# Exponentials of one PSUM bank in two halves, and of two banks in one operation, in a multi-query attention kernel

## The chip, the cores and the metric

The kernel runs on one core of a Trainium2 chip. The core has five engines with a queue of instructions each: TensorE (PE in the profile, with weight loads listed apart as PEld), VectorE (DVE), ScalarE (ACT), GpSimd (POOL) and SyncE (SP, which issues most of the transfers here). TensorE writes its products to PSUM, a memory of 128 partitions and eight banks of 512 float32 each; VectorE and ScalarE read them there and write to SBUF, the large on-chip memory. The metric is the device time of one execution in microseconds (us), lower being better.

## The reference, cut to what matters

A gated sum of two branches over one sequence of S = 2048 tokens of width D = 448:

```python
g = sigmoid((x * gate_w).sum(-1, keepdims=True))
a = A(x); b = B(x_b)
return g * a + (1 - g) * b

# A: multi-query attention, H = 16 heads of Dh = 28, one set of keys and values for all heads
q = (x @ wq).reshape(S, H, Dh)
k, v = x @ wk, x @ wv
p = softmax(einsum("qhd,kd->hqk", q, k) * Dh ** -0.5)
a = einsum("hqk,kd->qhd", p, v).reshape(S, H * Dh) @ wo

# B: spatial shift mixing and a feed-forward block
hs = shift4(gelu(layernorm(x) @ w1)) @ w2
x1 = x + hs
b = x1 + gelu(layernorm(x1) @ w3) @ w4      # 448 -> 1792 -> 448
```

All is float32. The change lies in the attention: the scores, the exponentials and the products with the values. 16 heads times 2048 queries times 2048 keys are 67 million exponentials.

## The kernel before, in words

Three stages follow each other. Stage 1 projects queries, keys and values (the queries wait in DRAM) and does the shift mixing. Stage 2 is the feed-forward block. Stage 3, from about 403 us to the end, is the attention and the output projection. The order of the instructions on every engine is the order in which the program writes them (a manual schedule); the semaphores between engines are set by the framework from what each instruction reads and writes.

**Attention.** The queries are in 16 units `u`: a block of 512 queries times a group of four heads. For one unit the 2048 keys come in 16 key tiles of 128. For one key tile, `scores` (L204) makes four products, one per head, in three rounds (high times high, low times high, high times low parts, to keep float32 precision). Each lands in a PSUM bank of its own: 128 keys by 512 queries. The four heads of a round run side by side on TensorE, each on 32 rows. The exponentials (`exps`, L257) read the banks and write the tile `p` in SBUF. `values` (L893) multiplies `p` with the values; it takes p as the moving operand, 256 queries at a time, and leaves the four heads' results in the four quarters of the partitions.

**The eight banks.** Four are single tiles, named `s0`, `s1`, `s2`, `s3_`; four form two pairs of banks, `pairs[0]` and `pairs[1]`. A pair is a tile of 128 x 2 x 512 read by one operation. From cycle to cycle `s0, s1` and `s2, s3_` change places.

**A cycle.** One pass through the main loop (index `c`, 128 of them) takes two key tiles. For TensorE it is written in this order:

1. scores of the first key tile into `s0`, `s1` and the two banks of `pairs[0]`;
2. scores of the second key tile into `s2`, `s3_` and the two banks of `pairs[1]`;
3. value products of the *previous* cycle's two tiles for queries 0 to 255, into the left half of `s0` (32 matmuls in all with step 4);
4. the same for queries 256 to 511, into the left half of `s1`;
5. usually one job (L844): half of an output projection of an earlier unit, into the right half of `s0`. In one cycle of each unit, row maxima of the next unit come between 3 and 4, into `pairs[0]` (L211).

For ScalarE the cycle before the change is: exponential of `s0` (`left`), of `s1` (`right`), of `s2`, of `s3_`, of `pairs[1]` (1024 columns, `both`), and then of the half of the first tile's `p` that VectorE has copied from `pairs[0]` to SBUF (L954), in place. That is six operations: four of 128x512 and two of 128x1024.

VectorE copies `pairs[0]` to SBUF, adds the value products to the running sums of the unit (`values_end`, L818; L814 the first time), once for step 3 and once for step 4, and adds the job's product (L860).

Step 3 writes to the bank `s0` that this cycle's first exponential reads, and step 5 writes to the bank that VectorE's first addition reads.

**Where the single banks come from.** Stages 1 and 2 use them too, through `mm_tile` (two buffers in turn, for the gate products of the feed-forward block among others) and `misc_tile` (one). `max_tile` gives the fourth. At the end of stage 2 they are made the four `singles`.

**Marked blocks.** In two cycles (`HINTS`, c = 68 and c = 110) the first exponential stands in a block of its own, which serves a hint for the later branch to the fallback path (that path recomputes everything with exact maxima, and isn't taken here).

Of the kernel before, what the change touches and what calls it, by code (L numbers as in the profile page):

```python
# [9 lines left out]
F32 = mybir.dt.float32  # L10
F32R = mybir.dt.float32r
BF16 = mybir.dt.bfloat16
AF = mybir.ActivationFunctionType
# [4 lines left out]
P = 128  # L18
# [11 lines left out]
SCALE = DH ** -0.5  # L30
# [12 lines left out]
def gated_mix_kernel(  # L43
# [12 lines left out]
    nc = tc.nc  # L56
# [3 lines left out]
    psA = ctx.enter_context(tc.tile_pool(name="psA", bufs=1, space=PSUM))  # L60
# [22 lines left out]
    nc.gpsimd.memset(vext[:, :, 0:1], 1.0)  # L83
    nc.gpsimd.memset(f32(kl), 1.0)

    def mm_tile(name):
        return psA.tile([P, 512], F32, tag="mm", bufs=2, name=name)

    def misc_tile(name):
        return psA.tile([P, 512], F32, tag="misc", bufs=1, name=name)  # L90

    def max_tile(name):
        return psA.tile([P, 512], F32, tag="mx", bufs=1, name=name)

    wps = misc_tile("warm_ps")
    for _ in range(20):
# [156 lines left out]
            for p in range(4):  # L253
                nc.sync.dma_start(rows[p], mrow[32 * p + 16 * k:32 * p + 16 * k + 16, :])

    def exps(p, heads, source=None):
        nc.scalar.activation(p[:, heads], p[:, heads] if source is None else source, AF.Exp, scale=SCALE)  # L257

    ctx2 = ExitStack()

# [1 line left out]
    with tc.tile_pool(name="s1b", bufs=1) as s1b, \  # L262
# [231 lines left out]
        q0 = first_queries()  # L494
# [172 lines left out]
    with tc.tile_pool(name="s2", bufs=1, reuse_waits="tile") as s2, \  # L667
# [35 lines left out]
        for b in range(NB):  # L703
            acc = [ps2.tile([P, 512], F32, tag="acc", bufs=4, name=f"acc_{b}_{t}") for t in range(4)]
            gs = {}
            for f in range(NF):
                if f == 9 and b + 1 < NB:
                    mv, rs = layernorm_stats(s2a, b + 1)
                if f == 10 and b + 1 < NB:
                    xt4 = big(f"xt4_{b + 1}")[:, 0:4 * D].rearrange("p (f t j) -> p f t j", f=NE, t=4)  # L710
                if f in (10, 11) and b + 1 < NB:
                    for t in (2 * f - 20, 2 * f - 19):
                        xn = s2a.tile([P, 512], F32, tag="xn", bufs=1, name=f"xn_{b + 1}_{t}")[:, 0:D]
                        layernorm_norm(b + 1, t, mv, rs, xn, xt4)
                if f == 11 and b + 1 < NB:
                    xt_write(b + 1, xt4)
                    ln_read(b + 1)
                gs[f] = w3_part(b, f)
                if b == 0 and f % 2 and f < 11:
                    split_w3((f + 3) // 2)  # L720
                    split_w4((f + 3) // 2)
                    if f == 1:
                        s2.tile([P, 48], F32, name="gap2")
                    if f < 9:
                        load_w34((f + 5) // 2, s2)
                if b == 1 and f == 0:
                    nc.gpsimd.tensor_tensor(gg, invE, gz, ALU.pow)
                    nc.vector.tensor_scalar(gg, gg, 1.0, None, op0=ALU.add)
                    nc.vector.reciprocal(gg, gg)
                    nc.vector.tensor_scalar(gi, gg, -1.0, 1.0, op0=ALU.mult, op1=ALU.add)  # L730
                if b == NB - 1 and f == 4:
                    weigh_x1(0, 4 * b)
                if b == 1 and f == 1:
                    nc.gpsimd.memset(khd, 0.0)
                    for j in range(4):
                        h = slice(32 * j, 32 * j + DH)
                        nc.gpsimd.tensor_copy(khd[h, j * MK:(j + 1) * MK], f32(kh_of[0])[h, 0:MK])
                    qr0 = s2a.tile([P, 512], F32, tag="xn", bufs=1, name="qr_0")
                    nc.gpsimd.memset(qr0, 0.0)
                    q_load(0, qr0)  # L740
                    nc.sync.dma_start(w4_late, w4[F - P:F, :])
                if b == 1 and f == 5:
                    q_high(0, qh0, ql0)
                    q_low(0)
                if f >= 2:
                    for t in range(4):
                        w4_part(f - 2, t, gs[f - 2], acc)
                        if b > 1 and t % 2 == 0 and f < NF - 1:
                            fill()
            if b == NB - 1:  # L750
                singles = [mm_tile("bank_0"), mm_tile("bank_1"), misc_tile("bank_2"), max_tile("bank_3")]
                scores(0, 0, singles)
                nc.scalar.activation(first, powt, AF.Exp)
                p_first = big("p_0_0").rearrange("p (j n) -> p j n", j=4)
                for j in range(4):
                    exps(p_first, slice(j, j + 1), singles[j].unsqueeze(1))
            for t in range(4):
                w4_part(NF - 2, t, gs[NF - 2], acc, NF - 2 if b == NB - 1 else NF - 1)
                if b + 1 < NB:
                    ln_split(b + 1, t, t + 1)  # L760
            for t in range(4):
                if b < NB - 1:
                    w4_part(NF - 1, t, gs[NF - 1], acc)
                xt = x1[:, 4 * b + t, :]
                nc.vector.tensor_add(xt, xt, acc[t][:, 0:D])
# [4 lines left out]
    with tc.tile_pool(name="s3", bufs=1, reuse_waits="tile") as s3, \  # L770
# [128 lines left out]
        left, right, both, front = slice(0, 1), slice(1, 2), slice(2, 4), slice(0, 2)  # L899
# [25 lines left out]
        for c in range(NC):  # L925
            u, i = divmod(c, NT // 2)
            k = 2 * c
            s0, s1, s2, s3_ = singles if c % 2 == 0 else singles[2:] + singles[:2]
            if c == 0:
                pb = score_tiles(u, 1, s2, s3_, s0, s1)  # L930
                for j, ps in enumerate((s2, s3_, s0, s1)):
                    exps(pb, slice(j, j + 1), ps.unsqueeze(1))
                pa = score_tiles(u, 2, *(q[:, h] for q in pairs for h in range(2)))
                nc.vector.tensor_copy(pa[:, front], pairs[0])
                for ps, n in zip((s2, s3_), JOBS_0):
                    run_jobs(ps, n)
                exps(pa, both, pairs[1])
                exps(pa, front)
                pairs.reverse()
                continue  # L940
            if c > 1:
                pa = score_tiles(u, 2 * i, s0, s1, pairs[0][:, 0], pairs[0][:, 1])
                with tc.block() if c in HINTS else nullcontext():
                    if c in HINTS:
                        tc.mark_branch_hint_location("redo", "LikelyTaken", HINTS[c])
                    exps(pa, left, s0.unsqueeze(1))
                exps(pa, right, s1.unsqueeze(1))
            if i == 2 and u == 0:
                q_begin(1)
            if i == 3 and u == 0:  # L950
                q_low(1)
                q_fetch(2)
            if 1 < c < NC - 1:
                nc.vector.tensor_copy(pa[:, both], pairs[0])  # L954
            elif c > 1:
                exps(pa, both, pairs[0])
            if i == 3 and later:
                later.pop(0)()
            if i == 1 and sums:
                norms.append(recip(*sums.pop()))  # L960
            if i == (3 if u == NU - 1 else 4) and norms:
                w = norms[0][0]
                norm(*norms.pop())
            if i == 5 and u + 2 < NU:
                q_begin(u + 2)
            if i == 6 and u + 2 < NU:
                q_low(u + 2)
                q_fetch(u + 3)
            pb = score_tiles(u, 2 * i + 1, s2, s3_, pairs[1][:, 0], pairs[1][:, 1])
            exps(pb, left, s2.unsqueeze(1))  # L970
            exps(pb, right, s3_.unsqueeze(1))
            exps(pb, both, pairs[1])
            if 1 < c < NC - 1:
                exps(pa, both)
            if u and i == (3 if u == NU - 1 else 4):
                jobs += [(wo_products, wo_add, (u - 1, t), cols) for t in range(4) for cols in halves]
            v = (c - 1) // (NT // 2)
            at_max = i == MAX_AT and u + 1 < NU
            q0, q1 = slice(0, 256), slice(256, 512)
            values((k - 2, k - 1), s0[:, q0], q0)  # L980
            values_end(v, s0[:, q0], q0)
            if at_max:
                max_part(u + 1, range(4), pairs[0][:, 0])
                later.append(lambda u=u: max_end(u + 1))
            elif i == MAX_AT:
                run_jobs(pairs[0][:, 0], 1)
            values((k - 2, k - 1), s1[:, q0], q1)
            adds = job_products(s0[:, q1], 0 if c in IDLE or c == 1 else 1)
            values_end(v, s1[:, q0], q1)
            job_adds(adds)  # L990
            if i == 0 and v < NU - 1:
                sums.append(sums_begin(v))
# [152 lines left out]
```

## Time and profile before

| what | value |
|---|---|
| time, median of 3 runs | 911.5 us (911.43 to 911.81) |
| span of the profiled execution, first to last instruction | 909.7 us |
| instructions | 24149 |
| TensorE matmul rows busy | 903.1 us, 99% |
| ScalarE busy | 632.6 us, 70% |
| VectorE busy | 515.8 us, 57% |
| granted TensorE clock, mean | 0.999 |
| attention, 128 cycles | about 403 to 899 us |
| ScalarE busy between 500 and 800 us | 99.64 to 99.75 us in each 100 us |

The profiled execution's time is given by its span; the runs' times include what lies before the first and behind the last instruction, and their median is 1.8 us above the span. How to read the rows: an instruction row of a timeline gives start and length in us, engine, line, operation, the tiles written and read, the shapes, how many were merged into the row, and in brackets how long the engine was idle before it and which instruction ended the idle time. PE's rows show matmuls in the pipeline, where several stand at once; PEld's rows show the loads of their weights, which go ahead of the matmul. A row of waits gives who waited, for whom, the sum in us, how many times, and the longest. ScalarE's operations overlap too: the next one starts before the end of the last.

### The profile page before, as it was taken

The page shows a single profiled execution, that of the slowest core. Times are in us where ns is not written, and L with a number is a line of the kernel's source. Part 1 is how long each engine was busy: PE and PEld are TensorE (multiplying, and loading weights), DVE is VectorE, ACT ScalarE, POOL GpSimd, SP SyncE. Part 2 cuts the span into 40 slices and gives each one's busy share as a digit, 9 for nine tenths or more (in the row PEclk, how much of TensorE's full clock was granted, in tenths as well). Part 3 has the DMA queues.
Part 4 walks back from the last instruction along what each step waited for, and adds up shares of the span by engine and source line. Part 5 has one row for each costly group of instructions (what it writes and reads, how often), then busy time and mean ns, then how long its engine had stood idle before and what let it go on. Part 6 is the DMA issues. An engine that isn't in the chain of part 4 may idle for free.

```text
span 909.7 us, 24149 instructions
## 1 busy us (share of the span) xinstructions
PE 903.1 (99%) x10360; PEld 626.8 (69%) x10360; DVE 515.8 (57%) x960; ACT 632.6 (70%) x1003; POOL 79.1 (9%) x116
## 2 busy tenths in 40 slices
PE   9999999999999999999999999999999999999998
PEld 6788888888888888875555555555555555555554
DVE  3665273631441531136766777676767667767665
ACT  5542444332132231269999999999999999999995
POOL 3243320200000520020000000000000000000000
PEclk9999999999999999999999999999999999999999
DMA  8832653120110120010000001000011000010001
GB/s 294 289 103 61 147 167 129 37 70 1 39 49 2 22 65 1 1 52 24 14 25 14 24 15 56 23 25 17 25 33 36 24 14 25 15 55 14 15 14 44
DMA packets 40726, 47.31 MB, mean 52 GB/s; under 512 B 10152, under 2 KB 28904, under 8 KB 40616
## 3 DMA queue, kind: packets, MB, share of 16 engines
q1 hardware_dynamic: 37448, 40.43, 15.2%
q10 hardware_dynamic: 3168, 5.31, 1.6%
q8 instruction: 82, 1.34, 0.6%
q14 instruction: 28, 0.23, 0.1%
HBM read 32.56 MB, written 11.67 MB: 49 GB/s over the span
## 4 chain that ended last, share of the span: by engine, by line
PE 97%; ACT 2%; DMA 1%; DVE 0%; issue 0%; SPq 0%
PE bank L893 26%; PE bank L204 20%; PE bank L844 6%; PE acc L701 5%; PE acc L699 5%; PE acc L700 5%; PE g L135 4%; PE g L137 4%; PE g L136 4%; PE pair L204 2%; ACT p L257 2%; PE hs L475 1%; PE hs L476 1%; PE g L138 1%; PE g L139 1%; PE h L136 1%
## 5 line engine op out<-in xcount | busy, mean ns | idle before, releaser
L257 ACT ACTIVATE p<-bank 128x512 f32<-128x512 f32 x514 | 265.9, 605 | 4.4 <-POOL pick L866 1.5
L893 PE MATMUL bank<-p,vext 128*32 128x256 f32 x4064 | 247.7, 382 | 1.0 <-ACT p L257 1.0
L893 PEld LDWEIGHTS bank<-p,vext 128*32 128x32 f32 x4064 | 117.9, 110 | 115.9 <-ACT p L257 53.0
L954 DVE COPY p<-pair 128x1024 f32<-128x1024 f32 x125 | 153.0, 1224 | 57.9 <-PE pair L204 40.9
L689 ACT ACTIVATE gh<-g 128x512 fp32r<-128x512 f32 x55 | 32.9, 598 | 181.7 <-PE g L139 181.7
L818 DVE TENSOR_TENSOR o<-o,bank 128x256 f32<-128x256 f32 x222 | 93.5, 421 | 80.4 <-PE bank L893 72.3
L257 ACT ACTIVATE p<-p 128x1024 f32<-128x1024 f32 x126 | 138.0, 1096 | 0.0
L257 ACT ACTIVATE p<-pair 128x1024 f32<-128x1024 f32 x129 | 136.8, 1060 | 0.0
L691 DVE TENSOR_TENSOR gl<-gf,gh 128x512 fp32r<-128x512 f32 x55 | 38.6, 702 | 164.9 <-ACT gf L690 164.9
L204 PE MATMUL bank<-qh,kh 32*128 32x512 f32 x514 | 114.8, 443 | 0.0
L204 PE MATMUL pair<-qh,kh 32*128 32x512 f32 x510 | 114.0, 443 | 0.0
L204 PE MATMUL bank<-qh,kl 32*128 32x512 f32 x514 | 101.8, 389 | 0.0
L204 PE MATMUL bank<-ql,kh 32*128 32x512 f32 x514 | 101.6, 390 | 0.0
L204 PE MATMUL pair<-qh,kl 32*128 32x512 f32 x510 | 101.3, 389 | 0.0
L204 PE MATMUL pair<-ql,kh 32*128 32x512 f32 x510 | 100.9, 389 | 0.0
L204 PEld LDWEIGHTS bank<-qh,kh 32*128 32x128 f32 x514 | 48.0, 182 | 61.3 <-issue 38.7
L701 PE MATMUL acc<-w4h,gl 128*128 128x448 f32 x220 | 80.7, 367 | 0.0
L699 PE MATMUL acc<-w4h,gh 128*128 128x448 f32 x220 | 80.2, 364 | 0.0
L700 PE MATMUL acc<-w4l,gh 128*128 128x448 f32 x220 | 79.8, 363 | 0.0
L844 PE MATMUL bank<-wof,on 128*32 128x224 f32 (+1 forms) x984 | 69.6, 357 | 0.0
L135 PE MATMUL g<-ah,w3h 128*128 128x512 f32 x168 | 65.4, 389 | 0.0
L136 PE MATMUL g<-al,w3h 128*128 128x512 f32 x168 | 65.4, 389 | 0.0
(206 smaller groups left out, 1394.1 us busy)
## 6 DMA issues: line engine op xcount, KB each, us to landing
qd<-qf ACTq DMA_DIRECT2D x15, 256.0 KB
rb<-rd SPq DMA_DIRECT2D x15, 256.0 KB
x<-in_x_dram SPq DMA_DIRECT2D x4, 896.0 KB
xd<-xt SPq DMA_DIRECT2D x16, 224.0 KB
w34raw<-in_w_dram SPq DMA_DIRECT2D x7, 512.0 KB
qr<-qd SPq DMA_DIRECT2D x64, 56.0 KB
w34raw<-in_w_dram SPq DMA_DIRECT2D x7, 448.0 KB
out_dram<-ot SPq DMA_DIRECT2D x14, 224.0 KB
```

Source lines behind the costliest of these rows:

```text
L135: nc.tensor.matmul(ps, wh[:, c, :], ah[:, c, :], start=(c == 0), stop=False)
L136: nc.tensor.matmul(ps, wh[:, c, :], al[:, c, :], start=False, stop=False)
L204: nc.tensor.matmul(ps[j], k[h, keys], q[h, :], start=(r == 0), stop=(r == 2), tile_position=(32 * j, 0))
L257: nc.scalar.activation(p[:, heads], p[:, heads] if source is None else source, AF.Exp, scale=SCALE)
L691: nc.vector.tensor_sub(gl, gf, f32(gh))
L699: nc.tensor.matmul(ps, gh[:, tok], w4h[i][:, k, :], start=(f == 0), stop=False)
L700: nc.tensor.matmul(ps, gh[:, tok], w4l[i][:, k, :], start=False, stop=False)
L701: nc.tensor.matmul(ps, gl[:, tok], w4h[i][:, k, :], start=False, stop=(f == stop))
L818: nc.vector.tensor_add(o, o, pv)
L844: nc.tensor.matmul(ps[32 * i:32 * i + 32, :], a[:, c:c + 32], w, start=start, stop=stop, tile_position=(0, 32 * i))
L893: nc.tensor.matmul(pv[32 * j:32 * j + 32, :], vext[:, kt, :], p_of[k][:, j, qs], start=(k == ks[0]), stop=(k == ks[-1]), tile_position=(0, ...
L954: nc.vector.tensor_copy(pa[:, both], pairs[0])
```

## The change

The four single banks become two tiles of two banks (`duo_0`, `duo_1`), of which `mm_tile`, `misc_tile` and `singles` are halves. In a cycle's ScalarE order, the first operation (bank `s0`, 512 queries) becomes two operations of 256 queries each, `q0` and `q1`. The third and the fourth (banks `s2` and `s3_` of the second key tile) become one operation over the two-bank tile that they form. The number of operations per cycle stays six: two of 128x256, one of 128x512, three of 128x1024. In the marked blocks only the first half remains inside; the second half follows the block. The last cycle reads `pairs[0]` directly as before.

```diff
+    duos = [psA.tile([P, 2, 512], F32, name=f"duo_{i}") for i in range(2)]
+    mm_turn = [0]
+
     def mm_tile(name):
-        return psA.tile([P, 512], F32, tag="mm", bufs=2, name=name)
+        mm_turn[0] += 1
+        return duos[0][:, 1 - mm_turn[0] % 2]
 
     def misc_tile(name):
-        return psA.tile([P, 512], F32, tag="misc", bufs=1, name=name)
-
-    def max_tile(name):
-        return psA.tile([P, 512], F32, tag="mx", bufs=1, name=name)
+        return duos[1][:, 0]
...
-    def exps(p, heads, source=None):
-        nc.scalar.activation(p[:, heads], p[:, heads] if source is None else source, AF.Exp, scale=SCALE)
+    def exps(p, heads, source=None, qs=slice(0, 512)):
+        nc.scalar.activation(p[:, heads, qs], p[:, heads] if source is None else source, AF.Exp, scale=SCALE)
...
-                singles = [mm_tile("bank_0"), mm_tile("bank_1"), misc_tile("bank_2"), max_tile("bank_3")]
+                singles = [d[:, h] for d in duos for h in range(2)]
...
             s0, s1, s2, s3_ = singles if c % 2 == 0 else singles[2:] + singles[:2]
+            duo = duos[1 - c % 2]
+            q0, q1 = slice(0, 256), slice(256, 512)
...
                 with tc.block() if c in HINTS else nullcontext():
                     if c in HINTS:
                         tc.mark_branch_hint_location("redo", "LikelyTaken", HINTS[c])
-                    exps(pa, left, s0.unsqueeze(1))
+                    exps(pa, left, s0[:, q0].unsqueeze(1), q0)
+                exps(pa, left, s0[:, q1].unsqueeze(1), q1)
                 exps(pa, right, s1.unsqueeze(1))
...
             pb = score_tiles(u, 2 * i + 1, s2, s3_, pairs[1][:, 0], pairs[1][:, 1])
-            exps(pb, left, s2.unsqueeze(1))
-            exps(pb, right, s3_.unsqueeze(1))
+            exps(pb, front, duo)
             exps(pb, both, pairs[1])
...
-            q0, q1 = slice(0, 256), slice(256, 512)
             values((k - 2, k - 1), s0[:, q0], q0)
             values_end(v, s0[:, q0], q0)
```

## The prediction

> **What bounds the kernel now.** I read the page's share table first, then the groups of instructions for the stretch 445 to 875 us (attention in its steady state), then the waits of that stretch, and then the timeline of two cycles at 609 us. On the page TensorE's matmul row is busy almost throughout. That alone decides nothing, since a matmul that stands in the pipeline counts as busy.
>
> ```profile
> span 909.7 us, 24149 instructions
> PE 903.1 (99%) x10360; PEld 626.8 (69%) x10360; DVE 515.8 (57%) x960; ACT 632.6 (70%) x1003; POOL 79.1 (9%) x116
> ```
>
> The waits between 445 and 875 us (engine and tile that waited, whom it waited for, us in total, times, longest) show where TensorE stands still:
>
> ```profile
> PEld bank L893 <- ACT p L257: 45.4, 110, 0.4
> PEld bank L204 <- issue: 34.3, 96, 0.4
> PEld bank L844 <- DVE o L818: 18.4, 83, 0.3
> ```
>
> One cycle of the loop handles two key tiles. The second row names no other engine ("issue" is time without a wait that the profile shows); the third is taken up below. 430 us hold 110 waits of the value products (L893) for an exponential, so there is one in every cycle and a cycle takes 430/110 = 3.91 us. The timeline of one cycle tells which exponential it is. The first row is the last operation of the cycle before. The single operations come from narrow windows; the row with x4 is the same four together.
>
> ```profile
> 608.08 1.09 ACT L257 ACTIVATE p<-p 128x1024 f32<-128x1024 f32 x1
> 608.72 0.40 PE L204 MATMUL pair<-qh,kl 32*128 32x512 f32 x2
> 609.14 0.60 ACT L257 ACTIVATE p<-bank 128x512 f32<-128x512 f32 x1
> 609.14 2.07 ACT L257 ACTIVATE p<-bank 128x512 f32<-128x512 f32 x4
> 609.42 0.39 PE L204 MATMUL bank<-qh,kl 32*128 32x512 f32 x1
> 609.64 0.59 ACT L257 ACTIVATE p<-bank 128x512 f32<-128x512 f32 x1
> 609.79 1.45 PEld L893 LDWEIGHTS bank<-p,vext 128*32 128x32 f32 x32 [0.41 <-ACT p L257]
> 610.11 0.61 ACT L257 ACTIVATE p<-bank 128x512 f32<-128x512 f32 x1
> 610.59 0.62 ACT L257 ACTIVATE p<-bank 128x512 f32<-128x512 f32 x1
> 611.07 1.06 ACT L257 ACTIVATE p<-pair 128x1024 f32<-128x1024 f32 x1
> 611.97 1.09 ACT L257 ACTIVATE p<-p 128x1024 f32<-128x1024 f32 x1
> 613.03 0.60 ACT L257 ACTIVATE p<-bank 128x512 f32<-128x512 f32 x1
> 613.68 0.16 PEld L893 LDWEIGHTS bank<-p,vext 128*32 128x32 f32 x8 [0.40 <-ACT p L257]
> ```
>
> The first key tile's scores end at 608.72 + 0.40 = 609.12. ScalarE starts on bank s0 at 609.14 and ends at 609.74. The value products, whose result goes into the left half of that same bank, load their first weights at 609.79, 0.05 us later. In the next cycle it is again 613.03 + 0.60 = 613.63 and 613.68. So the cycle is a ring: scores into s0, exponential of s0, value products into s0, output products, next scores. Whatever the exponential of s0 lasts longer or shorter, each cycle does too, as far as the rest of TensorE's work allows it.
>
> How much of that wait is real is seen where nothing has to be waited for. In an early cycle ScalarE was done with s0 at 406.33 + 0.60 = 406.93, long before the products:
>
> ```profile
> 406.33 0.60 ACT L257 ACTIVATE p<-bank 128x512 f32<-128x512 f32 x1
> 406.88 0.39 PE L204 MATMUL pair<-qh,kl 32*128 32x512 f32 x2
> 407.20 0.42 PE L893 MATMUL bank<-p,vext 128*32 128x256 f32 x4
> ```
>
> There the products start 407.20 − 406.88 = 0.32 us after the last scores. In the steady cycle it is 609.79 − 609.42 = 0.37. Only 0.05 us per cycle is lost to the exponential, though the wait row says 0.41.
>
> ScalarE itself has some room. From the operation on the tile in SBUF to the next cycle's first exponential are 609.14 − 608.08 = 1.06 us; where ScalarE is the one that is late, 417.98 − 417.03 = 0.95 us do:
>
> ```profile
> 417.03 1.09 ACT L257 ACTIVATE p<-p 128x1024 f32<-128x1024 f32 x1
> 417.98 1.12 ACT L257 ACTIVATE p<-bank 128x512 f32<-128x512 f32 x2
> ```
>
> **The change, part by part.** *Two halves in place of the first exponential.* The question is which of the halves the value products wait for. They write columns 0 to 255 of s0, and the second half reads columns 256 to 511 of the same bank. The kernel already has such a pair: the output products (L844) write columns 256 and up of s0, while VectorE (L818) has columns 0 to 255 to read.
>
> ```profile
> 610.99 0.42 DVE L818 TENSOR_TENSOR o<-o,bank 128x256 f32<-128x256 f32 x1
> 611.46 0.22 PEld L844 LDWEIGHTS bank<-wof,on 128*32 128x32 f32 x8 [0.22 <-DVE o L818]
> ```
>
> 610.99 + 0.42 = 611.41, and 0.05 us later L844 begins. It shares no column with L818, takes nothing that L818 makes, and still waits for it; the wait row above has it 83 times. So in this program order is kept by bank, not by column, and the value products will wait for the second half as well. The split then lengthens the ring by the cost of one more operation.
>
> The Trainium skill, "PSUM — Partial Sum Buffer", section "PSUM bank collisions raise a hardware error", says the same from the chip's side: two engines on one bank and the same 32 partitions at once is an error even at different columns, so one has to guard by bank. It speaks against the change; the trace's wait of L844 agrees.
>
> How much is it? No 128x256 exponential stands in the trace, so I take it from the two sizes that do. Start to start, operations of 512 follow each other at 610.59 − 610.11 = 0.48 us and one of 1024 is followed after 611.97 − 611.07 = 0.90. The 512 further elements take 0.42, so 256 take 0.21, and an operation has 0.48 − 0.42 = 0.06 us of its own. The first after a pause is followed after 0.50, 0.02 more. The first half is thus followed after 0.27 to 0.29 us, the second half lasts 0.59 − 0.21 = 0.38, and both end 0.65 to 0.67 after the start, where the single operation ended after 0.60. I take 0.06 us per cycle, the whole of one operation's own share.
>
> Both bounds: the least is 0.05. The most is what it would be if the halves did not overlap at all, which other operations of this kernel show (64 partitions, out of SBUF):
>
> ```profile
> 116.32 0.40 ACT L112 CAST w3h<-w34raw 64x256 fp32r<-64x256 f32 x1
> 116.74 0.41 ACT L113 CAST w3l<-w34raw 64x256 fp32r<-64x256 f32 x1
> ```
>
> The second starts 0.42 after the first, whose length is 0.40. Then the halves end 0.38 + 0.02 + 0.38 = 0.78 after the start: 0.18 more. That these two read one bank is no reason to expect it, for the two activations after the gate product also read one bank and overlap:
>
> ```profile
> 354.19 0.60 ACT L689 ACTIVATE gh<-g 128x512 fp32r<-128x512 f32 x1 [3.83 <-PE g L139]
> 354.69 0.59 ACT L690 ACTIVATE gf<-g 128x512 f32<-128x512 f32 x1
> ```
>
> The Trainium skill, "ScalarE: Activation LUTs", section "What ACT_TABLE_LOAD costs", gives 186 ns and 0.833 ns per element, of which back-to-back operations overlap by about 93 ns. By it one more operation is an estimated 0.093 us, and the sum below would be 11 us instead of 7. The trace is nearer to 0.06 at both sizes.
>
> *One operation for the second tile's two banks.* It takes away one start: two of 0.48 become one of 0.90, 0.06 us less. ScalarE's work per cycle is therefore what it was. But these operations come behind the gating one, and their results are used in the next cycle. Nothing waits for them at the end of the ring, so the 0.06 won here only goes to ScalarE's room of 0.11. The joint operation must wait for the scores of both banks. Those are complete at 609.42 + 0.39 = 609.81, and ScalarE gets there at about 610.11 + 0.05. It frees the first bank later, at about 610.16 + 1.06 = 611.22; the next scores into that bank start at 612.04:
>
> ```profile
> 612.04 0.49 PE L204 MATMUL bank<-qh,kh 32*128 32x512 f32 x2
> ```
>
> 0.8 us of cover, so this costs nothing. Without that cover scores would start late, by what the joint operation ends behind them.
>
> *The banks as halves of two tiles.* The feed-forward part uses the same two banks in turn, the score stage the same four. No operation, transfer or queue entry is added. If order is kept by bank, this costs nothing; what it costs otherwise is a rival below. The two marked blocks now hold the first half alone. After the later one ScalarE's operations follow without a gap (the second and third end 1.58 us after the first's start, 0.48 + 0.48 + 0.62), so I add nothing.
>
> ```profile
> 878.94 1.58 ACT L257 ACTIVATE p<-bank 128x512 f32<-128x512 f32 x3 [0.35 <-PE pair L204]
> ```
>
> **What is late next.** Value products 0.06 later move VectorE's additions and L844 with them, and the output products end 0.06 later, and so do the next scores. VectorE's copies wait for scores, ScalarE's room only grows. Nothing I see gives the time back.
>
> **The sum.** The value products' wait has 126 cases over the attention:
>
> ```profile
> PEld bank L893 <- ACT p L257: 53.0, 126, 0.7
> ```
>
> In some five early cycles like that at 417.98 ScalarE is late and the next start does not depend on TensorE, so I count 120. 120 × 0.06 = 7.2 us on the profiled span of 909.7, that is 916.9. The runs' median of 911.5 lies 1.8 us above this span; I keep that difference, and get 918.7 us.
>
> **The rivals.**
> 1. *Order by column.* If the products wait for the first half alone, that ends about 0.38 after its start, before TensorE is ready, and the products start at their own limit: 0.05 less per cycle, 120 × 0.05 = 6 us, 905.5 us. ScalarE's room of 0.11 would suffice. Against it stands L844's wait in 83 cases; for it, nothing in this trace. This is the other side, and it decides from the point where the products start ahead of the second half's end.
> 2. *Halves without overlap*: 120 × 0.18 = 21.6, 933 us. For it the 64-partition pair, against it all exponentials and the pair at 354 us.
> 3. *Order by tile.* If both banks of a joint tile count as one, the value products wait for s1's exponential too, which now ends at about 0.27 + 0.27 + 0.61 = 1.15 after the start instead of 0.60: 0.55 × 120 = 66 us, 977 us or more, as the feed-forward banks would be coupled as well. No row of the trace shows one bank of a two-bank tile written while the other is being read, so nothing speaks for or against.
> 4. *Nothing moves*: a later start of the products is taken up somewhere, 911.5 us. Against it: in two successive cycles they follow the exponential by the same 0.05 us, and TensorE has no other wait that could shrink.
>
> **How the numbers follow.** My forecast has 0.82, order by column 0.06, no overlap 0.04, order by tile 0.03, nothing moves 0.05. The forecast's own range is 0.05 to 0.09 us per cycle and a count of 115 to 126, with a little for what I have not seen: 916 to 924. The unknown price reaches toward rival 2 above and something given back below, so I widen it to 914 to 926, where about eight in ten lie. No change means within 0.2%, 1.8 us, about what a measurement of this kernel can tell. Faster is rival 1, 0.06; same is rival 4 and a price under a quarter of mine, 0.06; slower is the rest, 0.88.
>
> **What would show it.** In the changed profile there should be some 126 exponentials of 128x256 for each half, the second starting 0.27 to 0.29 us after the first and the value products 0.05 us after the end of the *second*. Their distance from the last scores should be 0.43 instead of 0.37, the cycle 3.97 instead of 3.91. Some 127 exponentials of 128x1024 from the joint tile stand in place of two of 128x512. If the products start before the second half ends, order is by column and I am wrong in sign; if they wait for the third operation, it is by tile; if the second half starts 0.4 after the first, the price was wrong.

## The result and the profile after

The changed kernel takes 1109.3 us (median, 1109.2 to 1109.7) against 911.5 us for the kernel before on the same chip: a ratio of 1.217, 95% interval 1.215 to 1.218. It is 198 us slower; 7 us were forecast.

The share table of the changed kernel's page:

```profile
span 1107.3 us, 24103 instructions
PE 971.1 (88%) x10360; PEld 613.7 (55%) x10360; DVE 519.5 (47%) x960; ACT 636.6 (57%) x1002; POOL 80.0 (7%) x116
```

The work is the same: as many matmuls, as many VectorE operations, ScalarE 636.6 us busy instead of 632.6 with one operation less. What grew is waiting. Four of the waits between 500 and 1000 us (engine and tile that waited, whom for, us in total, times, longest); the lines are one further down than before, so L894 is the value products, L819 VectorE's addition of them, L845 the job, L861 the addition of the job, L205 the scores and L258 the exponentials:

```profile
DVE o L819 <- PE duo L845: 126.3, 83, 1.6
PEld duo L894 <- DVE o L819: 84.5, 83, 1.1
PEld duo L894 <- ACT p L258: 66.3, 95, 0.7
PEld duo L205 <- DVE ot L861: 41.7, 95, 0.4
```

Of these only the third was in the profile before, but for two waits of the last kind, 0.4 us together. The value products now wait for VectorE, VectorE's additions wait for the job, and scores wait for the addition of the job. One cycle's timeline shows each (start, length, engine, line, tiles, and in brackets the idle time and what ended it):

```profile
702.84 0.50 PE L205 MATMUL duo<-qh,kh 32*128 32x512 f32 x2
703.32 0.45 DVE L861 SCALAR_TENSOR_TENSOR ot<-duo,gg,ot 128x224 f32<-128x224 f32 x1
703.81 0.18 PEld L205 LDWEIGHTS duo<-qh,kh 32*128 32x128 f32 x2 [0.44 <-DVE ot L861]
703.84 0.66 ACT L258 ACTIVATE p<-duo 128x256 f32<-128x256 f32 x2 [1.34 <-PE pair L205]
704.39 1.52 ACT L258 ACTIVATE p<-duo 128x512 f32<-128x512 f32 x2
705.04 1.07 PE L894 MATMUL duo<-p,vext 128*32 128x256 f32 x16 [0.26 <-ACT p L258]
706.24 0.42 DVE L819 TENSOR_TENSOR o<-o,duo 128x256 f32<-128x256 f32 x1 [0.53 <-ACT p L258]
706.71 1.07 PE L894 MATMUL duo<-p,vext 128*32 128x256 f32 x16 [0.60 <-DVE o L819]
707.60 0.56 PE L845 MATMUL duo<-wof,on 128*32 128x224 f32 x8
708.09 0.51 PE L205 MATMUL duo<-qh,kh 32*128 32x512 f32 x2
708.23 0.42 DVE L819 TENSOR_TENSOR o<-o,duo 128x256 f32<-128x256 f32 x1 [1.57 <-PE duo L845]
```

Read with the order of the program: the two halves of the exponential of s0 end at 703.84 + 0.66 = 704.50. The value products into s0 do not start then. They start at 705.04, 0.05 us after the exponential of **s1**, which starts at 704.39 and lasts 0.60 (the second row of ScalarE holds it and the joint operation, which starts at 704.87). The second part of the products, which goes into s1, waits until VectorE has read s0: 706.24 + 0.42 = 706.66, start at 706.71. VectorE's addition from s1 waits until the job has been written beside it into s0: 707.60 + 0.56 = 708.16, start at 708.23. s0 and s1 are now two banks of one tile, and whoever writes one of them waits for whoever uses the other. That is rival 3 of the prediction, with its sign and the kind of its mechanism, at three times its price.

The cycle is 708.09 − 702.84 = 5.25 us, where 3.91 were read before. The value products of the first cycles start at these times, before and changed:

```profile
403.47 0.42 PE L893 MATMUL bank<-p,vext 128*32 128x256 f32 x4
```

```profile
428.13 1.07 PE L894 MATMUL duo<-p,vext 128*32 128x256 f32 x16
```

So 24.7 us of the 197.6 us of span are lost ahead of the attention, where the projections of the first stage and the gate products of the feed-forward part share the same tiles, 169 us in the attention cycles (5.25 − 3.91 = 1.34, times 126), and the remaining 4 us behind the start of the last cycle's value products (18.4 us to the end of the span instead of 14.5). In the experiments below, one of the four runs of the last kernel had a granted clock of 0.75 and took 1195.5 us; it is left out of that kernel's time.

### The profile page after: what moved, and what is told of

It reads as the page before. It is cut to its first block, busy times and chain, and to the rows that moved or that the text cites. A ratio compares the mean times of both kernels' runs of the same rounds, so it can differ in the third digit from the quotient of the medians.

```text
span 1107.3 us, 24103 instructions
## 1 busy us (share of the span) xinstructions
PE 971.1 (88%) x10360; PEld 613.7 (55%) x10360; DVE 519.5 (47%) x960; ACT 636.6 (57%) x1002; POOL 80.0 (7%) x116
## 3 DMA queue, kind: packets, MB, share of 16 engines
q8 instruction: 82, 1.34, 0.5%
## 4 chain that ended last, share of the span: by engine, by line
PE 79%; ACT 11%; DVE 6%; issue 3%; DMA 1%; DVEq 0%; SPq 0%; ACTq 0%; POOL 0%
PE duo L894 21%; PE duo L205 18%; ACT p L258 9%; PE duo L136 5%; PE duo L845 5%; DVE o L819 4%; PE duo L137 4%; PE duo L138 4%; PE acc L702 4%; PE acc L700 4%; PE acc L701 4%; PE duo L140 1%; PE duo L139 1%; PE hs L476 1%; PE hs L477 1%
## 5 line engine op out<-in xcount | busy, mean ns | idle before, releaser
L894 PE MATMUL duo<-p,vext 128*32 128x256 f32 x4064 | 271.9, 385 | 109.4 <-DVE o L819 64.9
L258 ACT ACTIVATE p<-duo 128x256 f32<-128x256 f32 (+2 forms) x513 | 265.6, 603 | 171.2 <-PE pair L205 155.0
L894 PEld LDWEIGHTS duo<-p,vext 128*32 128x32 f32 x4064 | 106.0, 109 | 264.2 <-DVE o L819 112.9
L819 DVE TENSOR_TENSOR o<-o,duo 128x256 f32<-128x256 f32 x222 | 93.5, 421 | 264.1 <-PE duo L845 161.8
L258 ACT ACTIVATE p<-p 128x1024 f32<-128x1024 f32 x126 | 135.1, 1072 | 0.0
L258 ACT ACTIVATE p<-pair 128x1024 f32<-128x1024 f32 x129 | 134.0, 1039 | 0.0
L205 PE MATMUL duo<-qh,kh 32*128 32x512 f32 x514 | 126.3, 492 | 0.3
L205 PE MATMUL pair<-qh,kh 32*128 32x512 f32 x510 | 125.7, 491 | 0.0
L205 PEld LDWEIGHTS duo<-qh,kh 32*128 32x128 f32 x514 | 47.1, 181 | 99.7 <-DVE ot L861 50.5
L205 PE MATMUL pair<-qh,kl 32*128 32x512 f32 x510 | 100.8, 391 | 0.0
L205 PE MATMUL duo<-qh,kl 32*128 32x512 f32 x514 | 100.8, 390 | 0.0
L205 PE MATMUL duo<-ql,kh 32*128 32x512 f32 x514 | 100.7, 390 | 0.0
L205 PE MATMUL pair<-ql,kh 32*128 32x512 f32 x510 | 100.4, 390 | 0.0
L136 PE MATMUL duo<-ah,w3h 128*128 128x512 f32 x168 | 66.3, 395 | 9.4 <-ACT gf L691 9.4
L845 PE MATMUL duo<-wof,on 128*32 128x224 f32 (+1 forms) x984 | 70.1, 357 | 2.2 <-DVE ot L861 1.6
L137 PE MATMUL duo<-al,w3h 128*128 128x512 f32 x168 | 65.5, 390 | 0.0
```

The costliest lines, as they stand in the source:

```text
L136: nc.tensor.matmul(ps, wh[:, c, :], ah[:, c, :], start=(c == 0), stop=False)
L137: nc.tensor.matmul(ps, wh[:, c, :], al[:, c, :], start=False, stop=False)
L205: nc.tensor.matmul(ps[j], k[h, keys], q[h, :], start=(r == 0), stop=(r == 2), tile_position=(32 * j, 0))
L258: nc.scalar.activation(p[:, heads, qs], p[:, heads] if source is None else source, AF.Exp, scale=SCALE)
L819: nc.vector.tensor_add(o, o, pv)
L845: nc.tensor.matmul(ps[32 * i:32 * i + 32, :], a[:, c:c + 32], w, start=start, stop=stop, tile_position=(0, 32 * i))
```

## The experiments

Each kernel stands against the kernel before on the same chip (911.6 us). "Start to start" below is the distance between two starts in the same cycle, the median over 126 cycles, worked out from the start times in the trace.

| kernel | us | ratio to before, 95% interval |
|---|---|---|
| halves alone | 919.1 | 1.008 (1.007 to 1.010) |
| joint tiles alone | 1100.7 | 1.208 (1.206 to 1.210) |
| joint tiles and joint read | 1104.8 | 1.211 (1.209 to 1.213) |
| changed kernel, early buffers apart | 1095.8 | 1.202 (1.200 to 1.204) |
| order of s0 and s1 exchanged | 972.1 | 1.066 (1.065 to 1.068) |
| both parts in one bank | 1012.2 | 1.110 (1.108 to 1.112) |
| one joint tile of two | 1012.2 | 1.110 (1.108 to 1.113) |

**Halves alone.** The four single tiles as before; only the first exponential is split.

```diff
-                    exps(pa, left, s0.unsqueeze(1))
+                    exps(pa, left, s0[:, q0].unsqueeze(1), q0)
+                exps(pa, left, s0[:, q1].unsqueeze(1), q1)
                 exps(pa, right, s1.unsqueeze(1))
```

> The first exponential in two halves, everything else as before: four single tiles, separate reads. Theory (order is kept by whole tile, the joint tiles are the loss): the split alone costs what was priced for it, 0.06 us in each of some 120 cycles, 7 us, so 918.7 us, with the value products 0.05 us after the second half. Rival (the split itself is the loss): over 1000 us. Order by column inside a single tile would give 905.

It took 919.1 us, 7.5 more than before. The timeline of one cycle:

```profile
703.17 0.38 ACT L257 ACTIVATE p<-bank 128x256 f32<-128x256 f32 x1
703.17 0.66 ACT L257 ACTIVATE p<-bank 128x256 f32<-128x256 f32 x2
703.43 0.39 PE L204 MATMUL bank<-qh,kl 32*128 32x512 f32 x2
703.88 0.16 PEld L893 LDWEIGHTS bank<-p,vext 128*32 128x32 f32 x8 [0.48 <-ACT p L257]
```

The first half ends at 703.55, both at 703.83, and the products load at 703.88, after the second half, 0.06 later than where a single operation of 0.60 would have let them start. Within one bank order is kept across columns, and the price of one more operation is what was estimated. This half of the forecast stands; it just isn't where the time went.

**Joint tiles alone.** The allocation of the changed kernel, all operations of the kernel before.

```diff
-                    exps(pa, left, s0[:, q0].unsqueeze(1), q0)
-                exps(pa, left, s0[:, q1].unsqueeze(1), q1)
+                    exps(pa, left, s0.unsqueeze(1))
...
-            exps(pb, front, duo)
+            exps(pb, left, s2.unsqueeze(1))
+            exps(pb, right, s3_.unsqueeze(1))
```

(as a difference to the changed kernel)

> The four single banks as halves of two tiles, every operation as before (no halves, no joint read). Theory (order by whole tile): nearly the whole loss. The first two stages lose the 24.7 us that the changed kernel lost (its first value products start at 428.1 us instead of 403.5), and each attention cycle lasts 0.06 us less than the changed kernel's 5.25; 1109 - 126 x 0.06 = 1102 us. Rival (the joint read couples the two banks): 911 us here.

1100.7 us. Not one operation differs from the kernel before, and 189 us are lost. Its waits between 500 and 1000 us are those of the changed kernel:

```profile
DVE o L819 <- PE duo L845: 129.5, 85, 1.6
PEld duo L894 <- DVE o L819: 85.6, 84, 1.1
PEld duo L205 <- DVE ot L861: 42.2, 96, 0.4
```

**Joint tiles and joint read.** As the last, with the one operation over both banks.

```diff
-            exps(pb, left, s2.unsqueeze(1))
-            exps(pb, right, s3_.unsqueeze(1))
+            exps(pb, front, duo)
```

> The two joint tiles and the joint read of the second key tile's banks, but the first exponential whole. Theory (order by whole tile): the joint read frees nothing and costs nothing, 1102 us like the joint tiles without it. Rival (the joint read is the loss): 1102 us here and 911 us without it.

1104.8 us. The cycle is 5.20 us with the joint read and 5.19 without it, so in the attention the joint read neither costs nor gains anything, as expected. The 4 us more lie before it: the first full cycle's products start at 435.2 instead of 431.7 us. The two kernels do the same work there, but TensorE's granted clock differs in the first stage. These are the first 100 us (start, end, length; busy time of PE, PEld, DVE, ACT and POOL with their instructions; then the granted clock, 1.00 and 0.97, and the transfers) and the first and the eleventh matmul of one projection, of the joint tiles alone and then of this kernel:

```profile
0.00:100.00 100.00, 92.72 (x403) 72.22 (x404) 52.84 (x97) 40.98 (x66) 32.53 (x56) 1.00 0.56 173
27.84 0.50 PE L136 MATMUL duo<-ahk,wqh 128*128 128x512 f32 x1 [3.46 <-ACT qf L321]
30.24 0.39 PE L140 MATMUL duo<-ahk,wql 128*128 128x512 f32 x1
```

```profile
0.00:100.00 100.00, 91.94 (x386) 71.02 (x387) 52.13 (x97) 39.80 (x64) 32.49 (x56) 0.97 0.52 166
29.26 0.79 PE L136 MATMUL duo<-ahk,wqh 128*128 128x512 f32 x1 [4.23 <-ACT qf L321]
33.70 0.56 PE L140 MATMUL duo<-ahk,wql 128*128 128x512 f32 x1
```

The projection starts 1.4 us later, for a reason that is not shown, and takes 4.44 us instead of 2.40 from the first start to the last: 2.0 us are lost to the slower clock. Together that is 3.4 of the 3.5 us. The same shows within one kernel: of the four runs of the joint tiles alone, the one with the lowest mean clock (0.997) took 1103.4 us, the two at 1.000 took 1099.9 and 1100.0. The slow matmuls stand right behind TensorE's stop ahead of this projection; but the joint tiles alone have that stop too, of 3.46 us, and kept their clock, so what decides it is not shown. Against the changed kernel's 5.25 the whole first exponential is worth 0.06 us per cycle here too.

**The changed kernel with the early buffers apart.**

```diff
     def mm_tile(name):
         mm_turn[0] += 1
-        return duos[0][:, 1 - mm_turn[0] % 2]
+        return duos[1 - mm_turn[0] % 2][:, 0]
 
     def misc_tile(name):
-        return duos[1][:, 0]
+        return duos[1][:, 1]
```

> The changed kernel, but the two buffers that the first two stages use in turn lie in different joint tiles, and the third lies beside the second; the attention is as in the changed kernel. Theory (order by whole tile): neighbouring gate products no longer wait for each other's readers, nearly all of 24.7 us come back, 1085 us. Rival (the stages are slower for another reason, such as the fixed slices in place of buffers that rotate): 1109 us.

1095.8 us: 13.5 us come back, not 24.7. The busy time of the engines by stretches (start, end, length; then PE, PEld, DVE, ACT and POOL busy with their instructions; granted clock, share and rate of the transfers), first of the changed kernel, then of this one:

```profile
0.00:100.00 100.00, 92.49 (x396) 71.61 (x397) 52.16 (x97) 40.39 (x65) 32.51 (x56) 0.98 0.54 169
200.00:300.00 100.00, 95.30 (x456) 81.99 (x455) 32.82 (x60) 25.08 (x46) 1.21 (x2) 1.00 0.13 33
```

```profile
0.00:100.00 100.00, 92.58 (x394) 72.27 (x394) 51.94 (x97) 40.17 (x65) 32.45 (x56) 0.97 0.53 168
200.00:300.00 100.00, 100.00 (x483) 87.29 (x482) 32.95 (x61) 25.01 (x47) 1.21 (x2) 1.00 0.09 21
```

In the feed-forward part (200 to 300 us) everything is back: 100.00 and 483 matmuls, as many as the kernel before has there. In the first 100 us nothing is back. There the third buffer now lies beside one of the two, and the waits of its first 430 us are led by a new one of that kind, a projection that waits for VectorE's use of the third buffer:

```profile
PE duo L136 <- DVE w1raw L406: 5.0, 1, 5.0
```

The coupling had been moved to another neighbour; the expectation had counted only the two that take turns. The clock takes part as well: the eleven matmuls behind this wait take 4.43 us from the first start to the last, where the changed kernel takes 3.91 and the joint tiles alone take 2.40.

**Order of s0 and s1 exchanged.** Single tiles, the operations of the kernel before. The first part of the value products goes into s1 and the second into s0, so that the first waits for the second exponential: the first of the joint tiles' waits, alone.

```diff
-            values((k - 2, k - 1), s0[:, q0], q0)
-            values_end(v, s0[:, q0], q0)
+            values((k - 2, k - 1), s1[:, q0], q0)
+            values_end(v, s1[:, q0], q0)
...
-            values((k - 2, k - 1), s1[:, q0], q1)
-            adds = job_products(s0[:, q1], 0 if c in IDLE or c == 1 else 1)
-            values_end(v, s1[:, q0], q1)
+            values((k - 2, k - 1), s0[:, q0], q1)
+            adds = job_products(s1[:, q1], 0 if c in IDLE or c == 1 else 1)
+            values_end(v, s0[:, q0], q1)
```

> The kernel before with single tiles and all its operations, but the first value products go into bank s1 and the second into s0, and the job moves to s1's right half with them. Theory: it buys just one of the waits that a joint tile brings, that of the first value products for the second exponential. With the joint tiles and whole reads the products start 2.144 us after the first scores instead of 1.647, so 0.50 x 120 = 60 us, 971 us. Rival (that wait is hidden behind the late scores of the second key tile): under 920.

972.1 us, 60.6 more than before. From the first scores to the value products it is 2.13 us start to start, 1.65 before. The cost of that wait is not hidden by anything.

**Both parts in one bank.** Single tiles. The second part of the value products goes into the right half of s0 and so waits for VectorE's reading of the left half: the second wait, alone, made by one bank instead of one tile.

```diff
-            values((k - 2, k - 1), s1[:, q0], q1)
-            adds = job_products(s0[:, q1], 0 if c in IDLE or c == 1 else 1)
-            values_end(v, s1[:, q0], q1)
+            values((k - 2, k - 1), s0[:, q1], q1)
+            adds = job_products(s1[:, q0], 0 if c in IDLE or c == 1 else 1)
+            values_end(v, s0[:, q1], q1)
```

> The kernel before with single tiles, but both parts of the value products go into s0, the second into its right half; the job goes to s1. Theory: it buys just the other wait, that of the second part for VectorE's addition of the first, by order within one bank. With the joint tiles the second part starts 1.670 us after the first instead of 0.888, so 0.78 x 126 = 99 us, 1010 us. Rival (order by column inside a bank): no wait, 912 us or a little less.

1012.2 us, 100.6 more. The waits between 445 and 990 us and two starts from one cycle:

```profile
PEld bank L893 <- DVE o L818: 103.8, 102, 1.4
PE bank L893 <- DVE o L818: 59.8, 102, 1.0
```

```profile
703.55 1.07 PE L893 MATMUL bank<-p,vext 128*32 128x256 f32 x16
705.24 1.07 PE L893 MATMUL bank<-p,vext 128*32 128x256 f32 x16 [0.62 <-DVE o L814]
```

From the first to the second part it is 1.67 us start to start in the median (1.69 in the cycle shown), exactly what the joint tiles show, and 0.89 before. Again the first part's 256 columns and the second's do not overlap, and the order is kept.

The two waits bought one by one cost 60.6 and 100.6 us, 161 together. The joint tiles alone lose 5.19 − 3.89 = 1.30 us in the median cycle; from the first value products to the last, 126 cycles, they take 1079.86 − 426.93 = 652.9 us instead of 895.14 − 403.47 = 491.7, 161 us more. The third wait, that of the scores for the job's addition, adds almost nothing when both are there: scores whose last round starts 0.28 us late still end before the exponential of s1.

**One joint tile of two.** Only one pair of the single banks is a tile; the other two banks, with which the first two stages take turns, are single again.

```diff
-    duos = [psA.tile([P, 2, 512], F32, name=f"duo_{i}") for i in range(2)]
-    mm_turn = [0]
+    duo_1 = psA.tile([P, 2, 512], F32, name="duo_1")
...
-        mm_turn[0] += 1
-        return duos[0][:, 1 - mm_turn[0] % 2]
+        return psA.tile([P, 512], F32, tag="mm", bufs=2, name=name)
...
-        return duos[1][:, 0]
+        return duo_1[:, 0]
...
-                singles = [d[:, h] for d in duos for h in range(2)]
+                singles = [mm_tile("bank_0"), mm_tile("bank_1"), duo_1[:, 0], duo_1[:, 1]]
```

(and, as a difference to the changed kernel, the first exponential whole and the two banks read apart)

> Only the banks s2 and s3 of even cycles are one tile; the other two single banks stay two tiles, and all operations are as before. Theory (order by whole tile): stages 1 and 2 lose nothing (first value products at 407 us); in the 63 odd cycles the value products go into the joint tile and lose 1.30 us, in the 63 even ones the second scores wait for VectorE's last addition from it, 0.17 us late, of which 0.05 us were idle anyway: 63 x (1.30 + 0.12) = 89 us, 1001 us. If the late scores cost nothing: 993 us. Rival (a fixed cost of joint tiles anywhere): 911 or 1100.

1012.2 us, 11 more than expected. The mechanism holds: the cycles alternate, and the long ones show the two waits. What was priced too low is the even cycle. There the third wait is no longer behind a later one, and it costs more than its 0.17 us (this kernel's lines are one further up than in the kernel before: L203 the scores, L859 the addition of the job, L892 the value products):

```profile
707.11 0.44 DVE L859 SCALAR_TENSOR_TENSOR ot<-duo,gg,ot 128x224 f32<-128x224 f32 x1
707.60 0.18 PEld L203 LDWEIGHTS duo<-qh,kh 32*128 32x128 f32 x2 [0.44 <-DVE ot L859]
707.60 0.49 PE L203 MATMUL duo<-qh,kh 32*128 32x512 f32 x2
707.94 0.39 PE L203 MATMUL duo<-ql,kh 32*128 32x512 f32 x2
708.17 0.39 PE L203 MATMUL duo<-qh,kl 32*128 32x512 f32 x2
708.50 0.42 PE L892 MATMUL bank<-p,vext 128*32 128x256 f32 x4
```

After the wait the first round takes 707.94 − 707.60 = 0.34 us until the next one starts; the second takes 0.23. So the stop costs 0.17 + 0.11 = 0.28, of which 0.05 were idle before: about 0.23 instead of 0.12, 63 x 0.11 = 7 us more. In the median of the even cycles the products start 1.88 us after the first scores, where it was 1.65 before: the same 0.23. The other 4 to 5 us lie at both ends of the attention (its first full cycle's products are 3 us and its end 2 us later than those two offsets before), and were not followed further.

## Why the prediction was wrong

*What bounds the kernel*: right, and confirmed in sign and size. The ring from the scores into s0 through its exponential to the value products is the limit: 0.06 us added there came out as 7.5 us with the halves alone, and half a microsecond as 60.6 us with s0 and s1 exchanged. That only 0.05 us of the recorded wait of 0.41 was idle time does not follow from it: 0.06 more lengthens the cycle from 3.89 to 3.95 whatever part of the wait was idle. But the limit of about 0.32 from the last scores to the products, on which the 0.05 rests, came back where no exponential was late: 708.50 − 708.17 = 0.33 with one joint tile of two.

*Which half the products wait for*: right. With the halves alone they start 0.05 us after the second half, and the distance from the last scores is 0.06 more than before, 0.43 us start to start, as forecast. No part of the split's aim is reached as long as both halves are in one bank.

*The price of the split*: right. 7.2 us forecast, 7.5 measured. The second half ends 0.66 after the first's start; 0.65 to 0.67 was said. The figure of 93 ns, worked out from the Trainium skill's page "ScalarE: Activation LUTs", section "What ACT_TABLE_LOAD costs", would have given 11 us. The measured 0.06 decides.

*"The banks as halves of two tiles ... If order is kept by bank, this costs nothing"*: this step failed, and with it the sum. Order is kept by **tile**: with the tiles joined and no operation changed, the cycle went from 3.89 to 5.19 us. (No run separates the tile as such from the stretch of two banks that it covers.) The evidence on which it rested, L844's wait for L818, was real but could not tell the two apart: in the kernel before every such tile was one bank, so that a wait across columns of a bank is also a wait across columns of a tile. The prediction read "by bank" out of it, and the page of the Trainium skill that it named beside it ("PSUM — Partial Sum Buffer", section "PSUM bank collisions raise a hardware error") speaks of what the chip forbids and a program has to guard, not of what the framework of this program keeps in order. The program kept more in order than that rule asks for. No run here shows what the chip would do if two banks of one tile were used at once.

*One operation for two banks*: right that it costs and gains nothing in the cycle (5.20 against 5.19).

*Rival 3*: right in kind, given 0.03, and mis-sized. It was to cost 66 us, "or more": it counted only the first value products' wait for s1's exponential, at 0.55 us per cycle. That term was right: in the changed kernel the products start 2.21 us after the first scores instead of 1.65, 0.56 more, 0.50 of it without the split. It left out that VectorE's reading belongs to the tile as well: the second part's wait (0.78 us per cycle) was not there at all, and it is the larger. The two make up the 1.34 us of each cycle. Nor did it put a number on the feed-forward part (24.7 us with the first stage).

*Rivals 1, 2 and 4*: none occurred. The products never start ahead of the second half, the halves overlap (the second starts 0.28 after the first, 704.39 − 703.84 = 0.55 for both), and nothing took up the delay.

## What to carry to other kernels

Making two buffers one tile so that one operation can read both is not free even where nothing is added: every order that the framework keeps between users of a tile then holds between users of either half. Before joining, list who writes and who reads each half, and price every crossing. A wait seen between disjoint columns of a tile shows the grain of the order only down to the sizes that occur in the trace; where all tiles are one bank, tile and bank can't be told apart, and both prices belong into the forecast. And an operation is worth splitting for an earlier release only if the halves lie in different units of that grain.

## What the runs showed that was not expected

A wait stops TensorE for longer than the wait: after each stop before the second tile's scores, the first round took 0.34 us to the next instead of 0.23. It is what the first round behind the column-wise products takes in the kernel before (612.04 to 612.37), so it seems to belong to starting a row of matmuls, but no run took it apart.

A single wait's cost can be masked by a later one in the same ring. The scores' wait for the job's addition cost next to nothing with both tiles joined, and about 0.2 us per cycle where the cycle's other waits were gone.
